# Six key units of the second batch ahead of the expert's weights, and a later place in the order for readers of transferred data

## The chip, the cores and the metric

The kernel runs on one core of a Trainium2 chip. The metric is the device time of one execution in microseconds (us): the median of three runs of the kernel before is 1073.74 us (1071.4 to 1074.57). All rows of a profile in this document come from one profiled execution. PE is TensorE's matmul, PEld its weight load, DVE is VectorE, ACT ScalarE, POOL GpSimd, SP SyncE (which here only issues transfers). The granted clock (PEclk) is the share of TensorE's full speed that the throttle let through.

## The reference

Four batches of 11456 tokens with 128 channels. 49 agent vectors of each batch attend to the keys and average the values; each token then attends to the 49 averages. The result goes through a mixture of eight experts, of which each token takes the one with the largest gate logit.

```python
def _attn_ref(q, k, v, agents):
    a2k = sm(agents, k)                  # softmax of scale * a @ b.T
    agent_v = a2k @ v                    # 49 x 128 per batch
    q2a = sm(q, agents)
    return q2a @ agent_v

def _moe_ref(x, w_gate, w_output_gate, w1, w2):
    logits = x @ w_gate
    e_idx = np.argmax(logits, axis=1)
    ...
    for e in range(E):
        mask = e_idx == e
        h = np.maximum(x[mask] @ w1[e], 0.0)
        out[mask] = gate_w[mask, None] * eom[mask, e, None] * (h @ w2[e])
```

## The kernel before, in words

**Units and tiles.** A batch is cut into 12 units of 1024 tokens (the last has 192). Each batch has 12 key units (k), 12 value units (v) and 12 query units (q). A k unit is eight f32 products of the keys with the agents (`ks`), whose running maximum goes to DVE and whose scores are kept; a v unit is eight products `av` with the exponentials; a q unit is eight products `qs`, then maximum, exponential, a split into two f16 parts (`e16`), one transposing transfer into `x1`, four copies of 19 rows of `x1` into the four row groups of `x2`, and the gate logits `lg` from `x1`. When all values of a batch are averaged, `fold` finds the expert that most tokens take (`ei`), reads that number into SP, loads its two weight matrices (`w1t` in two halves, then `w2t`), multiplies the averages into the first (`aw`), scales and splits the results into `w` (the work of `first`) and the second matrix into `vv` (the work of `second`). The main loop then runs over 92 tiles of 512 tokens, 23 a batch: `h` products with `w` (`mm1`), `hh` on ACT and the remainder `hl` on DVE (`relu`), `y` products with `vv` (`mm2`), the sum into `os`, a multiplication on POOL and a store.

**The tokens of other experts** ("left" tokens) are gathered afterwards: `left_table` and `left_index` build their list with transfers into one buffer (`bigs` in the profile: rows of `ppid` by SP, rows of `cumd` and `efd` by gathers on POOL), DVE counts in that buffer, and 14 left tiles of 128 tokens each (two at first, then eleven of the first three batches, then one of the last batch) load their expert's weights and run `let`, `lx`, eight `lh` and eight `ly` products with ACT between them; a scatter on POOL writes them over the output. They are meant to run between the products of the last batch.

**What sets the order.** There is no order written by hand. The program is written out by generators ("streams") with priorities, and a planner, class `Clock`, keeps an estimated time for each engine and for each tile the time at which it is ready or read for the last time. `Clock.can` lets a request pass when its operands' estimated times have come, for some engines with an additional delay (`LATE`: 600 ns on PE, 800 on POOL, 2000 on SP, 0 on ACT and DVE), which holds only after the main loop has started and not where the writer is the asking engine. Up to now a transferred tile counted as written by the engine that issued its transfer. These estimates decide only in which order instructions stand on each engine; on the chip each engine runs its list in order and waits where an operand is not there, so an instruction placed too early holds up all behind it. `idle` fills an estimated gap of PE, before the main loop starts, with products on a constant (`warm`); next to the f32 products before the start stand fillers too (`beside`).

**Loads.** `loads` issues k, q and v units in the order of `ITEMS` into eight places of half a megabyte; a place comes free when the products of its unit are done. From item `FIRST_ITEMS` on (28 before) it also waits while `picking` is true, which `fold` sets before it reads the expert's number and clears once the expert's transfers are issued.

The lines that the change touches are `Clock.at` and `Clock.can`, the transfer branch of `Engine.emit` (line 174 on), `fold`, `second`, `order`, `FIRST_ITEMS`, the end of `main_stream`, and two pauses of the left tiles.

Of the kernel before, what the change touches and what calls it, by code (L numbers as in the profile page):

```python
# [47 lines left out]


class Clock:  # L50

# [6 lines left out]
    def __init__(self):  # L58
        self.vt = dict.fromkeys(("PE", "ACT", "DVE", "POOL", "SP", "DMA"), 0.0)
        self.ready, self.read, self.writer, self.before = {}, {}, {}, {}  # L60
        self.slots = [1, 2]
        self.pe = 0.0
        self.psum = set()

        self.apart = {"out"}
        self.recent = []
        self.started = False

    def now(self):
# [7 lines left out]

    def at(self, ins, outs=(), eng=None, late=0.0):

        t = 0.0  # L80
        for x in ins:
            if x.name not in self.apart:
                t = max(t, self.ready.get(x.name, 0.0) + (0.0 if self.writer.get(x.name) in (eng, "PE") else late))
        for x in outs:
            n = x.name
            if n in self.apart:
                continue
            if self.writer.get(n) != eng:
                t = max(t, self.ready.get(n, 0.0))
            t = max(t, self.read.get(n, 0.0), self.free_at(n))  # L90
        return t
# [5 lines left out]
    def can(self, req, prio):  # L97
        eng, ins, outs, kind = req
        now = self.now()
        t = self.at(ins, outs, eng, self.LATE[eng] if self.started and (prio > 0 or eng == "PE") else 0.0)  # L100
        if eng == "PE":
# [34 lines left out]
class Engine:  # L136
# [40 lines left out]
    def emit(self, op, ins, outs, a, k):  # L177
        if "dma" in op:
# [7 lines left out]
            for x in outs:  # L186
                c.ready[x.name] = max(c.ready.get(x.name, 0.0), q + (2500.0 if turned else 950.0))
                c.writer[x.name] = self.name
            for x in ins:
# [53 lines left out]
def agent_attention_top1_moe(ctx, tc, qT, kT, v, aT, wg, wo, w1, w2, cst, out):  # L243
# [422 lines left out]
    def fold(b):  # L666
# [36 lines left out]
        yield from SY.q.dma_start(w2t, w2[bass.ds(er, 1)].rearrange("a p f -> p (a f)"))  # L703
        picking[0] = False
        aw, marks = [], []
# [25 lines left out]
        release(mark)  # L731
        yield from SY.q.dma_start(avnd[b], avn[0:A])

    def gates(b, ad):
# [70 lines left out]
    def second(b, w2t):  # L805

        sq = wk.tile([P, 2], F32, name=f"sq2{b}", tag="sq")
        vvs = []
        for hf in range(2):
# [157 lines left out]
    def order():  # L967
        items = [("k", 0, u) for u in range(NU)] + [("q", 0, 0), ("q", 0, 1)] + [("v", 0, u) for u in range(NU)]
        for b in range(B):
            qs = [("q", b, u) for u in range(2, NU)]  # L970
            if b + 1 < B:
                qs += [("q", b + 1, 0), ("q", b + 1, 1)]
                ks = [("k", b + 1, u) for u in range(NU)]
                vs = [("v", b + 1, u) for u in range(NU)]
# [8 lines left out]
        return items  # L983

    MIX = [(3, 0)] * 4 + [(0, 0)] + [(0, 2)] * 6 + [(0, 0)]
    ITEMS = order()
    UNIT = {"q": q_unit, "k": k_unit, "v": v_unit}
    FIRST_ITEMS = 2 * NU + 4

# [102 lines left out]
    def main_stream():  # L1092
# [3 lines left out]
        while m2 < len(second_):  # L1096
# [23 lines left out]
            else:  # L1120
                idle()
        while streams:
            idle()
# [94 lines left out]
    def left_index(ph, i, n, nm, got=None):  # L1218
# [78 lines left out]
        for k in range(n):  # L1297
# [3 lines left out]
            if got:  # L1301
                got(k, clk.ready[big.name] + (4000.0 if n > 1 else 1000.0), ti, tg, ef, oa)
            yield from pause(1500.0 if n > 1 else 0.0)
# [18 lines left out]
    def pause(ns):  # L1322

        t = clk.now() + ns
        while clk.now() < t:
            yield None
# [63 lines left out]
    def left_static():  # L1390
# [3 lines left out]
        def fronts():  # L1394
            for i, (ph, k) in enumerate(todo):
# [4 lines left out]
                av, w1t, w2t = yield from left_load(ph, ti, kk, f"{ph}_{k}")  # L1400
                yield from pause(max(clk.ready[x.name] for x in (av, w1t, w2t)) - clk.now() + 2000.0)
                xs = yield from left_front(f"{ph}_{k}", ef, av)
# [119 lines left out]
```

## Time and profile before

| | before |
|---|---|
| median of three runs | 1073.74 us (1071.4 to 1074.57) |
| the profiled execution's own time | 1073.62 us |
| its span | 1071.6 us |
| its mean granted clock | 0.984 |
| PE busy | 1033.2 us |
| DVE busy | 859.9 us |
| ACT busy | 592.6 us |
| POOL busy | 275.2 us |
| bytes moved | 147.13 MB |

The span runs from the first to the last instruction; 2.0 us of the execution's own time lie around it. A busy PE isn't a PE at its peak: at half the granted clock a product takes longer and PE still counts as busy, so a stretch is to be read with both columns, busy time and PEclk. In the rows of a timeline the columns are start, duration, engine, line, operation, output<-input, shape and count, and in brackets the idle time just before and what ended it. Nearly all instructions are written from one helper line (L193), so rows are told apart by tile names, whose numbers are left out. An f32 product shows as two passes (x2).

### The profile page before, as it was taken

The numbers are of one execution on the slowest core, as the hardware profiler recorded it, in microseconds if no ns is written. First come the engines' busy times: TensorE is split into PE (matmuls) and PEld (weight loads), VectorE is DVE, ScalarE is ACT, GpSimd is POOL, SyncE is SP. The second block draws the span as 40 slices with busy tenths as digits, with TensorE's granted clock in tenths as the row PEclk, the third lists the DMA queues.
The fourth block names the chain that finished last, engine by engine and source line by source line (L and its number), as shares of the span: only waits on it lengthen the run. The fifth ranks groups of instructions, "written<-read, shape, count | busy, mean of one in ns | idle before, by whom it ended". The sixth has DMA issues, their size and how long they took to land. (4 is left out here: it accounts for less than half of the span.)

```text
span 1071.6 us, 27654 instructions
## 1 busy us (share of the span) xinstructions
PE 1033.2 (96%) x10671; PEld 840.9 (78%) x10671; DVE 859.9 (80%) x2344; ACT 592.6 (55%) x1396; POOL 275.2 (26%) x440
## 2 busy tenths in 40 slices
PE   9989899999999999999999999999899999999996
PEld 9977777788788877778788788777677676788885
DVE  2738699888988898888988888989989978877551
ACT  2325456565755665556755665556645554655552
POOL 0301123222121232232121232321123263521121
PEclk9999899999999999999999999999999998999998
DMA  8785854444557444453466544446232732644430
GB/s 293 231 213 156 193 117 146 125 122 136 133 141 197 141 134 112 119 147 116 111 185 166 153 125 119 129 123 171 73 75 56 168 92 78 149 136 130 131 124 28
DMA packets 108818, 147.13 MB, mean 137 GB/s; under 512 B 61128, under 2 KB 71548, under 8 KB 108682
## 3 DMA queue, kind: packets, MB, share of 16 engines
q1 hardware_dynamic: 107338, 143.83, 48.4%
q0 software_dynamic: 1344, 1.49, 0.8%
q8 instruction: 85, 1.39, 0.5%
q14 instruction: 51, 0.42, 0.1%
HBM read 91.86 MB, written 35.17 MB: 119 GB/s over the span
## 5 line engine op out<-in xcount | busy, mean ns | idle before, releaser
L193 PE MATMUL y<-vv,hh 128*128 128x256 f16 (+1 forms) x2880 | 593.0, 275 | 4.3 <-DVE w L193 3.1
L193 PE MATMUL y<-vv,hl 128*128 128x128 f16 (+1 forms) x2880 | 532.7, 220 | 3.3 <-DVE hl L193 2.5
L193 DVE SCALAR_TENSOR_TENSOR hl<-h,hh 128x512 f16<-128x512 f32 (+1 forms) x736 | 447.0, 667 | 85.3 <-ACT hh L193 84.2
L193 ACT ACTIVATE hh<-h 128x512 f16<-128x512 f32 (+1 forms) x736 | 372.2, 591 | 231.3 <-PE h L193 231.0
L193 PEld LDWEIGHTS <-hh 128*128 128x128 f16 (+1 forms) x2880 | 284.7, 99 | 67.0 <-issue 37.1
L193 PEld LDWEIGHTS <-hl 128*128 128x128 f16 (+1 forms) x2880 | 320.7, 112 | 10.9 <-DVE hl L193 6.2
L193 PE MATMUL h<-x_ld,w 128*128 128x512 f16 (+1 forms) x1472 | 289.4, 379 | 12.1 <-DVE hl L193 11.5
L193 PEld LDWEIGHTS <-w 128*128 128x128 f16 x1472 | 98.3, 103 | 105.0 <-issue 84.7
L193 POOL TENSOR_TENSOR os<-os,smt 128x512 f32<-128x512 f32 (+1 forms) x92 | 94.3, 1025 | 234.8 <-issue 168.9
L193 ACT COPY ys<-y 128x256 f32<-128x256 f32 x180 | 67.4, 374 | 99.6 <-PE y L193 97.4
L193 PEld LDWEIGHTS qs<-at,q_ld 128*128 128x128 f32 x720 | 112.0, 190 | 7.0 <-DVE km_m L193 0.3
L193 PE MATMUL qs<-at,q_ld 128*128 128x50 f32 x720 | 114.0, 245 | 0.0
L193 PE MATMUL ks<-at,k_ld 128*128 128x50 f32 x720 | 111.4, 257 | 2.2 <-DMA k_ld<-kT 2.2
L193 PEld LDWEIGHTS ks<-at,k_ld 128*128 128x128 f32 x720 | 109.2, 195 | 5.5 <-DMA k_ld<-kT 3.1
L193 PE MATMUL av<-ev,v_ld 128*128 128x50 f32 x720 | 110.7, 251 | 0.0
L193 PEld LDWEIGHTS av<-ev,v_ld 128*128 128x128 f32 x720 | 107.6, 191 | 1.8 <-ACT ev L193 0.2
L193 DVE TENSOR_TENSOR os<-y,ys 128x256 f32<-128x256 f32 x180 | 75.0, 417 | 30.3 <-ACT ys L193 22.4
L193 POOL TENSOR_TENSOR e<-ef,e 128x392 f16<-128x392 f32 (+1 forms) x48 | 41.8, 870 | 151.9 <-ACT e L193 93.4
L193 POOL TENSOR_TENSOR ev<-S,km_o 128x400 f32<-128x400 f32 (+1 forms) x44 | 41.1, 935 | 150.7 <-PE av L193 108.6
L193 POOL TENSOR_SCALAR smt<-lT,i 128x8 f32<-128x8 f32 (+1 forms) x48 | 14.8, 309 | 130.6 <-DVE lT L193 109.9
L193 PEld LDWEIGHTS <-idle_x 128*128 128x128 f16 x305 | 45.9, 158 | 2.7 <-DVE idle_x L193 1.1
L193 PE MATMUL lh<-lxs,lw 128*128 128x128 f32 x224 | 42.9, 276 | 0.0
(200 smaller groups left out, 1041.3 us busy)
## 6 DMA issues: line engine op xcount, KB each, us to landing
q_ld<-qT SPq DMA_DIRECT2D x44, 512.0 KB
v_ld<-v SPq DMA_DIRECT2D x44, 512.0 KB
out<-os SPq DMA_DIRECT2D x88, 256.0 KB
k_ld<-kT SPq DMA_DIRECT2D x43, 512.0 KB
lw<-w SPq DMA_DIRECT2D x28, 512.0 KB
efd<-ef SPq DMA_DIRECT2D x44, 200.0 KB
x_ld<-x_ld SPq DMA_DIRECT2D x176, 38.0 KB
w1t<-w SPq DMA_DIRECT2D x8, 256.0 KB
```

What stands on the lines that cost most here:

```text
L193: return getattr(self.eng, op)(*a, **k)
```

## The change

Five things are changed.

1. **Order of loads.** Six k units of batch 1 (`PRE = 6`) stand in `ITEMS` directly behind the values of batch 0, and `FIRST_ITEMS` is 32, so that they are loaded and scored without waiting for the expert. Before, `q0_2` and one k unit stood there.
2. **End of picking.** `picking` is cleared by a stream of its own, `picked`, when the planner expects `w2t` to have arrived, not when its transfer is issued.
3. **Order of the weights' preparation.** In batch 0 `second` begins when both parts of `w` have been written out.
4. **A transfer is a writer of its own.** A transferred tile's writer is now "DMA". After the start every reader of such a tile is placed 1500 ns (`LANDS`) behind the estimated arrival, on DVE and ACT too; at the end of the main loop this margin becomes 0. Since "DMA" is never the asking engine, the planner also lets a second transfer into the same tile wait for the first one's estimated arrival: the two halves of `w1t` and of the first k unit, the four copies into `x2`, the two parts of `wgo`, the rows gathered into the left tokens' buffer. No such wait is in the program itself; only the places in the order change. `lg` is asked for only after the fourth copy into `x2` has been issued (`q_rest`).
5. **Pauses of the left tiles** are 2000 ns shorter, or 1000 where one tile is gathered alone.

```diff
+LANDS = 1500.0
...
-    def at(self, ins, outs=(), eng=None, late=0.0):
+    def at(self, ins, outs=(), eng=None, late=None):
...
-                t = max(t, self.ready.get(x.name, 0.0) + (0.0 if self.writer.get(x.name) in (eng, "PE") else late))
+                w = self.writer.get(x.name)
+                if w == "DMA" and late is not None:
+                    more = self.margin
+                else:
+                    more = 0.0 if w in (eng, "PE") else late or 0.0
+                t = max(t, self.ready.get(x.name, 0.0) + more)
...
-        t = self.at(ins, outs, eng, self.LATE[eng] if self.started and (prio > 0 or eng == "PE") else 0.0)
+        t = self.at(ins, outs, eng, (self.LATE[eng] if prio > 0 or eng == "PE" else 0.0) if self.started else None)
...
-                c.writer[x.name] = self.name
+                c.writer[x.name] = "DMA"
...
-        picking[0] = False
+        spawn(picked(w2t), -1)
...
+    def picked(w2t):
+
+        yield from pause(clk.ready[w2t.name] - 950.0 - clk.now())
+        picking[0] = False
...
+        while b == 0 and len(state[b]["w"]) < 2:
+            yield None
...
+        items += [("k", 1, u) for u in range(PRE)]
...
-                ks = [("k", b + 1, u) for u in range(NU)]
+                ks = [("k", b + 1, u) for u in range(0 if b > 0 else PRE, NU)]
...
+    PRE = 6
...
-    FIRST_ITEMS = 2 * NU + 4
+    FIRST_ITEMS = 2 * NU + 8
...
+        clk.margin = 0.0
...
-                got(k, clk.ready[big.name] + (4000.0 if n > 1 else 1000.0), ti, tg, ef, oa)
+                got(k, clk.ready[big.name] + (2000.0 if n > 1 else 0.0), ti, tg, ef, oa)
...
-                yield from pause(max(clk.ready[x.name] for x in (av, w1t, w2t)) - clk.now() + 2000.0)
+                yield from pause(max(clk.ready[x.name] for x in (av, w1t, w2t)) - clk.now())
```

Three places show how the order moves. Line numbers differ because lines were added; the numbers at the ends of names are running numbers of buffers.

**SP's list between the values of batch 0 and its expert** (k1_0 is the first key unit of batch 1, x10_1 and x20_1 are x1 and x2 of batch 0's query unit 1, ei0 the expert's number). Before:

```order
L193 DMA q0_2_ld_737<-qT 128x1024
L193 DMA x20_0_ld_651<-x10_0_ld_634 19x1024 x4
L193 DMA_TRANSPOSE x10_1_ld_751<-e16_1_84 128x8x128
L193 DMA k1_0_ld_769<-kT 128x1024
L193 DMA x20_1_ld_757<-x10_1_ld_751 19x1024 x4
L696 TENSOR_LOAD ei0_929
L193 ISA
L193 DMA w1t0_938<-w1 128x512
L193 ISA
L193 DMA w1t0_938<-w1 128x512
L193 ISA
L193 DMA w2t0_941<-w2 128x1024
```

After, where four more key units, k1_0 to k1_3, and the first two of the four copies into x20_0 stand ahead of these rows:

```order
L203 DMA k1_4_ld_882<-kT 128x1024
L203 DMA k1_5_ld_902<-kT 128x1024
L203 DMA x20_0_ld_697<-x10_0_ld_687 19x1024 x2
L203 DMA_TRANSPOSE x10_1_ld_952<-e16_1_84 128x8x128
L706 TENSOR_LOAD ei0_971
L203 ISA
L203 DMA w1t0_982<-w1 128x512
L203 ISA
L203 DMA w1t0_982<-w1 128x512
L203 ISA
L203 DMA w2t0_1039<-w2 128x1024
```

The key units and the second transposing transfer now stand directly ahead of the expert's number, and the copies into x2 are no longer one group of four but are spread between loads. On PE the scores of k1_0 to k1_3 and five of the eight of k1_4 now stand ahead of the first `aw`; before, only q0_2 and k1_0 stood there. At the very beginning of PE's list 17 `warm` products now stand between the second and the third key unit, where there were none, and between the values and the start the `warm` products are 14 where there were 29.

**DVE's reading of the eleven gathers for the left tokens** (`bigs0_2<-bigs0_2,lppxs0_2` reads the eleven gathered rows; hl82_0 is a remainder of tile 82, os75 the output of tile 75). DVE before:

```order
L193 SCALAR_TENSOR_TENSOR hl76_4_16026<-h76_1_0_16002,hh76_4_16025 128x512
L193 SCALAR_TENSOR_TENSOR hl76_5_16029<-h76_1_1_16010,hh76_5_16028 128x512
L193 SCALAR_TENSOR_TENSOR hl76_6_16031<-h76_1_2_16014,hh76_6_16030 128x512
L193 SCALAR_TENSOR_TENSOR hl76_7_16033<-h76_1_3_16019,hh76_7_16032 128x512
L193 TENSOR_TENSOR os75_16005<-y75_1_16038,ys75_1_16087 128x256
L193 TENSOR_TENSOR bigs0_2_15045<-bigs0_2_15045,lppxs0_2_15567 128x990
```

DVE after:

```order
L203 SCALAR_TENSOR_TENSOR hl82_0_16919<-h82_0_0_16903,hh82_0_16918 128x512
L203 SCALAR_TENSOR_TENSOR hl82_1_16922<-h82_0_1_16908,hh82_1_16921 128x512
L203 SCALAR_TENSOR_TENSOR hl82_2_16924<-h82_0_2_16910,hh82_2_16923 128x512
L203 SCALAR_TENSOR_TENSOR hl82_3_16926<-h82_0_3_16912,hh82_3_16925 128x512
L203 TENSOR_TENSOR os81_16975<-y81_0_16896,ys81_0_16976 128x256
L203 TENSOR_TENSOR bigs0_2_15386<-bigs0_2_15386,lppxs0_2_16231 128x990
```

POOL's list around the last of these gathers, before:

```order
L193 TENSOR_TENSOR os74_15703<-os74_15703,smt3_2_14862 128x512
L193 DMA bigs0_2_15045<-cumd0_100,lrus0_2_15685 128x90
L193 TENSOR_SCALAR smt3_6_15996<-lT3_6_15991,i123_13761 128x8
L193 COPY ef3_6_15472<-lT3_6_15991 128x8
L193 TENSOR_TENSOR oht_1_96<-oh3_6_15959,ndom3_13423 128x8x8
L193 DMA bigs0_2_15045<-cumd0_100,lrus0_2_15685 128x90
L193 DMA out<-bigs0_0_14369,ltu0_0s0_0_14909 34368x128
L193 DMA bigs0_2_15045<-cumd0_100,lrus0_2_15685 128x90
L193 TENSOR_TENSOR os75_16005<-os75_16005,smt3_3_15231 128x512
```

POOL after:

```order
L203 DMA bigs0_2_15386<-cumd0_100,lrus0_2_16376 128x90 x2
L203 TENSOR_TENSOR os79_16631<-os79_16631,smt3_5_15909 128x512
L203 DMA bigs0_2_15386<-cumd0_100,lrus0_2_16376 128x90 x3
L203 TENSOR_TENSOR e16_2_85<-ef3_10_16848,e16_2_85 128x8x49
L203 CAST e16_2_85<-ef3_10_16848 128x8x30
L203 TENSOR_TENSOR os80_16814<-os80_16814,smt3_5_15909 128x512
L203 TENSOR_TENSOR os81_16975<-os81_16975,smt3_6_16084 128x512
```

Before, the last gather stood ahead of tile 75's multiplication on POOL, and DVE read the rows directly behind tile 75's last sum. Now the last gather stands between the multiplications of tiles 79 and 80, and DVE reads the rows in tile 82, more than a tile later; the whole chain of the left tokens stands about five tiles later in the last batch.

**The end of PE's list** (y91 is the last tile of the main loop; in lh0_12_1 the numbers are phase, left tile and half, and lh1_0 is the one left tile of the last batch). Before, the last rows ahead of the end:

```order
L193 MATMUL ly1_0_19147<-lw21_0_18937,lh1_0_0_19126 128x128
L193 LDWEIGHTS hl91_7_19042
L193 MATMUL y91_0_19100<-vv3_1_13658,hl91_7_19042 96x128
L193 MATMUL ly1_0_19147<-lw21_0_18937,lh1_0_0_19126 128x128 x3
L193 MATMUL ly1_0_19147<-lw21_0_18937,lh1_0_1_19143 128x128 x4
```

After:

```order
L203 MATMUL y91_0_19042<-vv3_1_13692,hl91_7_18972 96x128
L203 MATMUL ly0_11_19076<-lw20_11_18875,lh0_11_1_19072 128x128 x2
L203 MATMUL lx0_12_19102<-let_sb0_12_19096,lav0_12_19021 128x128
L203 MATMUL lh0_12_0_19130<-lxs0_12_19111,lw10_12_19023 128x128 x4
L203 MATMUL lh0_12_1_19137<-lxs0_12_19111,lw10_12_19023 128x128 x4
L203 MATMUL ly0_12_19145<-lw20_12_19025,lh0_12_0_19135 128x128 x4
L203 MATMUL ly0_12_19145<-lw20_12_19025,lh0_12_1_19142 128x128 x4
L203 MATMUL let1_0_19154<-kc_71,bigs1_0_18502 49x128
L203 MATMUL lx1_0_19162<-let_sb1_0_19156,lav1_0_19124 128x128
L203 MATMUL lh1_0_0_19166<-lxs1_0_19164,lw11_0_19126 128x128 x4
L203 MATMUL lh1_0_1_19173<-lxs1_0_19164,lw11_0_19126 128x128 x4
L203 MATMUL ly1_0_19180<-lw21_0_19128,lh1_0_0_19171 128x128 x4
```

Before, seven products of the last left tile stood behind the last product of the main loop; now nearly all of the last two left tiles stand there.

More of the change, by code (lines that the diff above doesn't have):

```diff
@@ L67, in __init__ @@
         self.started = False
+        self.margin = LANDS
     def now(self):
```

## The prediction

> **What bounds the kernel now.** I read the page's first two parts, then the waits of PE and DVE, then tables by stretch around each wait, then the timeline there. The page first: busy time by engine, and the granted clock in 40 slices of 26.8 us.
>
> ```profile
> PE 1033.2 (96%) x10671; PEld 840.9 (78%) x10671; DVE 859.9 (80%) x2344; ACT 592.6 (55%) x1396; POOL 275.2 (26%) x440
> PEclk9999899999999999999999999999999998999998
> ```
>
> PE bounds the whole: of 1071.6 us only 38.4 are idle, part of them before the first load lands and behind the last product. A new order cannot shorten the products, so what it can win are PE's gaps and the half clock that follows them. The waits of PE, largest first (total, times, longest):
>
> ```profile
> PE h L193 <- DVE hl L193: 11.5, 33, 3.6
> PE lg L193 <- DMA x_ld<-e: 3.7, 1, 3.7
> PE y L193 <- DVE w L193: 3.1, 1, 3.1
> PE ks L193 <- DMA k_ld<-kT: 2.2, 1, 2.2
> ```
>
> Four places carry most of it. The table by stretch shows busy times and clock there, and the left tokens' stage as a whole (800 to 840):
>
> ```profile
> core 0: us, PE busy (x) PEld busy (x) DVE busy (x) ACT busy (x) POOL busy (x), PEclk, DMA share, GB/s
> 76.00:86.00 10.00, 10.00 (x74) 9.37 (x73) 7.39 (x19) 5.85 (x12) 1.51 (x2) 0.66 0.89 340
> 126.00:134.00 8.00, 6.57 (x51) 4.72 (x52) 3.12 (x14) 2.83 (x8) 0.00 (x0) 0.59 0.78 256
> 752.00:760.00 8.00, 7.15 (x47) 4.82 (x47) 6.61 (x22) 4.36 (x11) 1.23 (x2) 0.79 0.05 17
> 798.00:808.00 10.00, 8.29 (x64) 5.13 (x62) 8.64 (x25) 2.85 (x7) 1.69 (x2) 0.83 0.33 78
> 884.00:896.00 12.00, 9.31 (x56) 5.29 (x56) 9.44 (x22) 2.65 (x6) 0.76 (x1) 0.72 0.02 7
> 800.00:840.00 40.00, 36.55 (x358) 26.45 (x358) 36.69 (x108) 21.77 (x52) 13.11 (x22) 0.96 0.27 63
> ```
>
> A stretch at clock c costs its length times (1 - c) beside its gap, where PE has work throughout: 76 to 86 lost 10 x 0.34 = 3.4 us although PE was busy in all of it, 126 to 134 lost 8 x 0.41 = 3.3.
>
> **Part by part: the start.** ACT's copies of scores in the opening and the steps from the expert's number to the first `y` (columns: start, duration, engine, line, operation, count, and in brackets the idle time before and its releaser):
>
> ```profile
> 14.30 0.49 ACT L193 COPY S<-ks 128x400 f32<-128x400 f32 x1 [1.65 <-PE ks L193]
> 16.44 0.49 ACT L193 COPY S<-ks 128x400 f32<-128x400 f32 x1 [1.65 <-PE ks L193]
> ...
> 63.83 0.15 DVE L193 TENSOR_SCALAR ei<-gm 128x1 int32<-128x1 f32 x1
> 65.93 0.94 SPq L193 DMA_DIRECT2D w1t<-w  x2
> 67.51 0.33 SPq L193 DMA_DIRECT2D w2t<-w  x1
> 69.17 2.81 PE L193 MATMUL aw<-w1t,avd 128*128 128x512 f32 x6 [0.20 <-DMA w1t<-w]
> 71.82 0.50 PE L193 MATMUL mw_r<-sq,ones 128*128 128x1 f32 x4
> 74.23 0.63 ACT L193 ACTIVATE vv<-w2t 128x512 f16<-128x512 f32 x1 [3.84 <-DMA w2t<-w]
> 75.53 0.42 PE L193 MATMUL ks<-at,k_ld 128*128 128x50 f32 x2 [2.25 <-DMA k_ld<-kT]
> 82.75 2.24 PE L193 MATMUL warm<-idle_x 128*128 128x256 f16 x10
> 85.03 0.38 PE L193 MATMUL h<-x_ld,w 128*128 128x512 f16 x1
> 87.72 0.27 PE L193 MATMUL y<-vv,hh 128*128 128x256 f16 x1
> ```
>
> In the opening ACT waits for PE and a unit takes 16.44 - 14.30 = 2.14 us, so more fillers there lengthen it. The order has 17 more, and two more beside them; at half clock a `warm` took 0.224 us (2.24 / 10), so 0.11 at full clock: 19 x 0.11 = 2.1 us. The expert's number moves from 63.83 to 66.0, the issue of `w1t` from 65.93 to 68.1. It landed 3.24 us after its issue (69.17), so 71.3 now, or up to 3 us later if the last two key units (two of 512 KB at the 340 GB/s of the row 76 to 86) still fill the queue. PE meanwhile has k1_0 to k1_3 and five eighths of k1_4, 4.6 x 2.14 = 9.9, and 1 us of other products: it comes to `aw` at about 74.3, so that even a late `w1t` is hidden. By 71.82 - 69.17 = 2.65 before and some 2.2 now (nothing else of PE lies between), `mw_r` moves from 71.82 to 76.5, 4.7 us later. Against that, ACT's 3.84 us wait for `w2t` goes, and `second` stands behind `w`: with ACT free for the halves of `w`, I get the first `h` at 84.3 and the first `y` at about 88 against 87.72. The new wait of `second` holds back only `vv` on ACT; behind it stands the first `y`, and that is in the 88.
>
> What has been gained by then is work done ahead. Six k units and 3/8 of a q unit are through, where five units were. A f32 product in the main loop costs PE 0.16 us:
>
> ```profile
> 120.52 0.32 PE L193 MATMUL ks<-at,k_ld 128*128 128x50 f32 x2
> 120.68 0.22 PE L193 MATMUL y<-vv,hl 128*128 128x128 f16 x1
> ```
>
> That is 8 x 0.16 = 1.3 us a unit, so 1.4 units are 1.8 us less in the main loop. Sum of the start: +0.3 - 1.8, taken as **-1**. Ends: -4, if ACT's whole 3.84 us is won; +3.4, if another gap brings the half clock of 76 to 86 into the part that now decides.
>
> On that clock the Trainium skill ("TensorE: Matmul & The Clock Gate", "Part 1: The HAM clock gate (the "warmup" mystery)") says that the gate falls to half only after an idle window of about 3.4 us. By this trace a gap of 2.25 us, at 75.53, was enough. By the page the start would carry no such risk and the upper end would be 0; by the row it stays.
>
> **Part by part: `lg` behind the first `x1` of the main loop.** Here the transfer was read too early by far:
>
> ```profile
> 119.03 2.29 SPq L193 DMA_TRANSPOSE x_ld<-e  x1
> 127.43 0.24 PE L193 MATMUL lg<-gs,x_ld 128*128 128x36 f16 x2 [3.68 <-DMA x_ld<-e]
> ```
>
> It landed 8.4 us after its issue, and PE stood 3.68 us. `lg` is now asked for after four copies that the planner spaces out (about 2.3 us each), plus 1.5 us of margin: some 8 us later in PE's list, which exceeds 3.68. The gap goes, and with it most of the half clock after it (of 3.3 us in the row 126 to 134 I take 2.5, as part lies in the gap itself): **-6.2**. At the worst the planner finds other work to put too early and nothing is won: 0.
>
> **The expert of batch 3** (752.85, row "PE y <- DVE w", 3.12 us). The half clock in 752 to 760 is 8 x 0.21 = 1.7, together 4.8. The two halves of `w1t` are spread, and more `y` now stand ahead of those that need the new `vv`. The wait is for DVE's `w`, not a transfer, so not all of it need go: **-3**, between -4.8 and 0.
>
> **The left tokens' tables** (800 and 884). The waits of DVE and of PE in the two stretches:
>
> ```profile
> DVE bigs L193 <- DMA out<-os: 3.4, 1, 3.4
> ...
> PE h L193 <- DVE hl L193: 1.7, 4, 1.0
> ...
> DVE bigs L193 <- DMA bigs<-cumd,lrus: 6.2, 1, 6.2
> ...
> PE h L193 <- DVE hl L193: 3.8, 2, 3.6
> ```
>
> DVE stands before the gathered rows, with PE's next `hl` queued behind it. On PE the two cost 1.7 + 3.8 of gap and 10 x 0.17 + 12 x 0.28 = 5.1 of clock: 10.6. But DVE is the full engine of this stage (36.69 us of 40 in 800 to 840), so no more comes back than DVE's own idle time, 3.4 + 6.2 = 9.6. DVE now reads the second set more than a tile after its last gather: **-9.5**, between -12 and -3 (only the first one's wait).
>
> **The end.** The left tokens now come about five tiles later, and two left tiles stand behind the last product of the main loop, where seven products stood:
>
> ```profile
> 1054.41 0.27 ACT L193 COPY lxs<-lx 128x128 f32<-128x128 f32 x1 [1.26 <-PE lx L193]
> ...
> 1059.19 1.78 PE L193 MATMUL ly<-lw,lh 128*128 128x128 f32 x14
> 1061.06 0.37 ACT L193 ACTIVATE bigs<-ly,bigs 128x128 f32<-128x128 f32 x1 [1.30 <-PE ly L193]
> ```
>
> A product is 1.78 / 7 = 0.254 us. A left tile alone is 16 of these, 4.1 us, and with the copies between (two of 0.27, an `lh` on ACT, `let`, `lx`) some 5.3: two are 10.7 against 2.3 before (1059.13 to 1061.43). About 26 products, 6.7 us, leave the main loop for it. 10.7 - 2.3 - 6.7 = 1.7, and with gaps between small products the clock may fall (2 us more): **+2.7**, between +1.7 and +3.7.
>
> **New waits.** The order changes everywhere; the trace before has none of the gaps it may bring. By the nearest rows a gap with its clock costs 4.8 to 6.2. I allow one small one, **+3**, between 0 and +8.
>
> **Sum.** The profiled execution took 1073.62 us (1071.6 of span, 2.0 around it), as the median of 1073.74. 1073.6 - 1 - 6.2 - 3 - 9.5 + 2.7 + 3 = 1059.6, so **1060**.
>
> **The rivals.**
> *Some waits go, others come* (1066 to 1071). For it: 11.5 us of PE's waits on `hl` are 33 small ones, which no margin on transfers touches; a reader moved back meets the next engine. Then -6 for `lg`, -3 for the left tokens, +2.7 and +3 or more remain.
> *It doesn't do what it says* (1070 to 1077). A margin of 1.5 us is small against a landing of 8.4, as at 119.03; where the estimate is off by more than the margin, a reader waits just as before at its new place, and the end's +2.7 cancels the rest. Against it: at both places by name the new order has more than the margin between.
> *Slower: the chain to `x2` starves the main loop* (1080 to 1100). The copies went out together:
>
> ```profile
> 94.61 2.48 SPq L193 DMA_DIRECT2D x_ld<-x_ld  x4
> ```
>
> Now they stand apart on SP, with loads between that wait for places. `h` needs all four. If the chain's lead over `h`, one or two tiles of 10.6 us (1059 - 85 over 92), falls under the some 7 us which spreading adds (4 x 2.3 - 2.5), each of the first units costs a stall of up to 7 and 3 of half clock; one to three such units less the gains give 1080 to 1100. Against it: in PE's waits above no `h` stands behind a transfer.
> *More than I take* (below 1051): the left tokens' whole 10.6, batch 3's 4.8, the start's 4, no new wait.
>
> **How the numbers follow.** The forecast (1051 to 1066) gets 0.50, more than that 0.05, the first rival 0.20, no effect 0.14, the slower one 0.11. A measurement of this kernel can tell about 0.3%, 3.2 us, from no change: faster is below 1070.5, slower above 1077. Faster: 0.50 + 0.05 + 0.18 = 0.73; within: 0.02 + 0.13 = 0.15; slower: 0.01 + 0.11 = 0.12. The range leaves out the slower rival, the case below 1051 and 0.04 of "no effect": **1051 to 1074**, which takes in the bounds of the terms, save all of them at one end together.
>
> **What would show it.** Right: no wait of PE for `x1` over 1 us and a clock over 0.95 near 120 to 135; no DVE wait over 2 us for `bigs`; `ei` near 66, first `y` between 85 and 91; about 10 us between the last main-loop `y` and the last `ly`. Wrong: `h` waiting for `x_ld` in the first twenty tiles; a new gap over 3 us with a clock near 0.5 behind it; `aw` waiting over 3 us for `w1t`; PE's waits in sum still above 15 us.

## The result, and the profile after

The changed kernel takes 1047.78 us (median of 4 runs, 1047.25 to 1048.62), the kernel before beside it 1074.15 (4 runs, 1071.4 to 1076.06): a ratio of 0.9757, 95% interval 0.9734 to 0.978. It is faster, as forecast, but by 26 us and not 14, and it lies below the range's low end of 1051. The profiled execution took 1047.73 us, its span is 1046.0.

The page of the changed kernel, parts 1 and 2, busy time by engine and the granted clock in 40 slices:

```profile
PE 1021.1 (98%) x10690; PEld 834.0 (80%) x10690; DVE 871.6 (83%) x2344; ACT 591.4 (57%) x1396; POOL 273.2 (26%) x440
PEclk9999999999999999999999999999999999999998
```

PE is busy 12.1 us less, with nothing left out: the same products ran at full clock, where some ran at half before. PE's idle time in the span fell by 13.5 us (38.4 to 24.9). The waits of PE that are left, the three largest (total, times, longest), and DVE's largest:

```profile
PE h L203 <- DVE hl L203: 3.6, 17, 0.2
PE y L203 <- DVE qz L203: 3.1, 4, 0.9
PE warm L203 <- DVE idle_x L203: 1.1, 1, 1.1
...
DVE hl L203 <- ACT hh L203: 45.5, 59, 2.5
```

No wait of PE for a transfer is left, nor DVE's for `bigs`, and none of PE's is longer than 1.1 us. DVE waited 84.2 us for `hh` before; that it waits 39 us less was not forecast.

Where the time went is read from both traces cut at the same places: at the first `h` of each batch and at the end of PE's last product. The kernel before, by stretch (length, busy times and counts, clock):

```profile
0.00:85.03 85.03, 80.95 (x809) 76.58 (x810) 41.76 (x121) 24.35 (x55) 13.60 (x28) 0.96 0.81 248
85.03:329.90 244.87, 237.41 (x2505) 191.62 (x2504) 213.21 (x596) 142.93 (x340) 58.96 (x105) 0.99 0.53 140
329.90:562.59 232.69, 230.33 (x2469) 187.00 (x2468) 204.48 (x549) 140.97 (x330) 57.51 (x97) 1.00 0.50 139
562.59:793.46 230.87, 225.72 (x2380) 179.82 (x2378) 205.82 (x566) 138.39 (x322) 56.35 (x95) 0.99 0.47 126
793.46:1060.97 267.51, 258.77 (x2519) 205.88 (x2517) 194.65 (x515) 145.62 (x348) 87.79 (x118) 0.98 0.41 114
1060.97:1071.56 10.59, 0.00 (x0) 0.00 (x0) 0.00 (x0) 0.37 (x1) 1.00 (x1) 0.66 0.06 16
```

The changed kernel, the same six:

```profile
0.00:84.41 84.41, 82.50 (x858) 78.45 (x859) 40.27 (x115) 23.71 (x55) 12.56 (x26) 1.00 0.78 227
84.41:318.71 234.30, 230.88 (x2476) 187.75 (x2476) 218.81 (x586) 142.88 (x339) 59.42 (x104) 1.00 0.59 155
318.71:549.72 231.01, 229.20 (x2469) 186.24 (x2468) 212.04 (x550) 140.16 (x331) 57.10 (x96) 1.00 0.51 140
549.72:774.57 224.85, 222.40 (x2370) 177.98 (x2369) 210.11 (x570) 136.99 (x323) 55.24 (x92) 1.00 0.50 129
774.57:1037.23 262.66, 256.10 (x2527) 203.53 (x2525) 190.38 (x527) 147.26 (x350) 87.87 (x121) 1.00 0.40 115
1037.23:1045.96 8.73, 0.00 (x0) 0.00 (x0) 0.00 (x0) 0.37 (x1) 0.97 (x1) 0.68 0.03 7
```

Length less PE busy is PE's gap. From stretch to stretch the lengths change by -0.6, -10.6, -1.7, -6.0, -4.9 and -1.9, together -25.6. Gaps ahead of PE's last product fell from 27.8 to 16.2 us; the half clock there, summed from the records of the clock (half of 27.3 us), fell from 13.7 us to nothing. Gap and half clock are 25.3 of the 25.6.

The places that the prediction named, in the changed kernel. The start:

```profile
66.96 0.14 DVE L203 TENSOR_SCALAR ei<-gm 128x1 int32<-128x1 f32 x1
...
67.84 1.35 SPq L203 DMA_DIRECT2D w1t<-w  x2
...
74.50 1.94 PE L203 MATMUL aw<-w1t,avd 128*128 128x512 f32 x4
76.28 0.50 PE L203 MATMUL mw_r<-sq,ones 128*128 128x1 f32 x4
...
84.41 1.35 PE L203 MATMUL h<-x_ld,w 128*128 128x512 f16 x8
...
87.16 0.27 PE L203 MATMUL y<-vv,hh 128*128 128x256 f16 x1 [0.15 <-DVE vv L203]
```

`aw` does not wait for `w1t`, and the steps stand within a microsecond of the forecast (66.0, 68.1, 74.3, 76.5, 84.3, 88). The wait of `lg`: a transposing transfer behind the start of the main loop, and the first `lg` that reads what it brings:

```profile
113.91 1.27 SPq L203 DMA_TRANSPOSE x_ld<-e  x1
131.10 0.21 PE L203 MATMUL lg<-gs,x_ld 128*128 128x36 f16 x2
```

The trace leaves the units' numbers out, so they are counted along the lists of SP and PE: this is unit 3. It is read 17.2 us after the issue; the `lg` at 115.61, close behind the transfer, still read unit 2, issued at 98.44. The wait of before was unit 4's, the third that the main loop issues: its `lg` was reached 4.7 us behind the issue (127.43 - 3.68 - 119.03), and the data came 8.4 us behind it. Now unit 4 is issued at 130.35 and read at 142.66, 12.3 us later, without a wait. Over all 48 units the shortest time from issue to first reader is 12.1 us, where it was 4.8. And the end, first before, then after (the store of the last tile, then the last scatter of left tokens):

```profile
1060.98 0.33 SPq L193 DMA_DIRECT2D out<-os  x1
...
1063.54 1.00 POOL L193 DMA_INDIRECT out<-bigs,ltg_0s  x1 [2.59 <-SPq L1457]
```

```profile
1037.32 0.37 ACT L203 ACTIVATE bigs<-ly,bigs 128x128 f32<-128x128 f32 x1 [1.30 <-PEq L1479]
1037.96 0.97 POOL L203 DMA_INDIRECT out<-bigs,ltg_0s  x1 [4.45 <-ACT bigs L203]
```

Before, the scatter waited 2.59 us for the store of the main loop's last tile, which it may overwrite. Now that store is 8 us old when the last left tile is done, and the scatter follows ACT at once.

### The profile page after: what moved, and what is told of

It is laid out like the page before. It is cut to its first block, busy times and chain, and to the rows that moved or that the text cites. A ratio compares the mean times of both kernels' runs of the same rounds, so it can differ in the third digit from the quotient of the medians.

```text
span 1046.0 us, 27720 instructions
## 1 busy us (share of the span) xinstructions
PE 1021.1 (98%) x10690; PEld 834.0 (80%) x10690; DVE 871.6 (83%) x2344; ACT 591.4 (57%) x1396; POOL 273.2 (26%) x440
## 5 line engine op out<-in xcount | busy, mean ns | idle before, releaser
L203 DVE SCALAR_TENSOR_TENSOR hl<-h,hh 128x512 f16<-128x512 f32 (+1 forms) x736 | 447.1, 667 | 49.3 <-ACT hh L203 45.5
L203 PE MATMUL h<-x_ld,w 128*128 128x512 f16 (+1 forms) x1472 | 284.7, 376 | 4.8 <-DVE hl L203 3.6
L203 PE MATMUL ks<-at,k_ld 128*128 128x50 f32 x720 | 107.8, 255 | 0.4 <-DVE os L203 0.4
L203 PEld LDWEIGHTS ks<-at,k_ld 128*128 128x128 f32 x720 | 104.5, 190 | 2.8 <-DVE os L203 1.6
L203 POOL TENSOR_TENSOR e<-ef,e 128x392 f16<-128x392 f32 (+1 forms) x48 | 41.4, 862 | 150.5 <-ACT e L203 137.4
L203 DVE TENSOR_REDUCE m<-ks 128x50 f32<-128x400 f32 (+1 forms) x44 | 23.8, 541 | 25.3 <-ACT S L203 25.0
L203 ACT COPY S<-ks 128x400 f32<-128x400 f32 (+1 forms) x48 | 22.7, 476 | 36.0 <-PE ks L203 35.9
```

Source lines behind the costliest of these rows:

```text
L203: return getattr(self.eng, op)(*a, **k)
```

## The experiments

All were timed against the kernel before on the same chip, 4 to 10 runs each (the kernel before 7 to 17); since that kernel's median moved between 1071.8 and 1074.7 us, ratios are compared. The table gives the ratio with its interval and, from each profile, the lengths of the six stretches, the half clock ahead of PE's last product, and the time of PE behind the main loop's last `y`. The profiled execution is one of the runs and not always near their median: e4's took 6.6 us more than the median in the table, e14's 4.2 and e3's 2.7 more, e12's 4.6 less. The stretches of these four are to be read with that.

| kernel | us | ratio (95%) | opening | batch 0 | 1 | 2 | 3 | end | half clock | behind last y |
|---|---|---|---|---|---|---|---|---|---|---|
| before | 1074.15 | 1 | 85.0 | 244.9 | 232.7 | 230.9 | 267.5 | 10.6 | 13.7 | 1.6 |
| changed | 1047.78 | 0.9757 (0.9734-0.9780) | 84.4 | 234.3 | 231.0 | 224.9 | 262.7 | 8.7 | 0 | 10.6 |
| e1 | 1058.02 | 0.9865 (0.9821-0.9910) | 85.3 | 237.2 | 231.0 | 224.8 | 268.7 | 8.7 | 3.4 | 28.6 |
| e2 | 1080.77 | 1.0076 (1.0047-1.0106) | 83.9 | 244.8 | 232.7 | 230.8 | 271.7 | 12.2 | 12.0 | 0 |
| e3 | 1063.66 | 0.9911 (0.9883-0.9940) | 84.2 | 239.5 | 231.9 | 226.0 | 271.0 | 11.9 | 6.8 | 0.3 |
| e4 | 1069.01 | 0.9978 (0.9954-1.0002) | 85.2 | 236.9 | 234.8 | 232.6 | 272.0 | 12.2 | 13.7 | 0 |
| e5 | 1059.04 | 0.9868 (0.9839-0.9897) | 79.2 | 239.0 | 232.0 | 226.8 | 267.3 | 12.2 | 3.4 | 0 |
| e6 | 1074.52 | 1.0014 (0.9986-1.0043) | 81.9 | 247.8 | 233.7 | 230.7 | 265.0 | 12.2 | 12.0 | 0 |
| e7 | 1061.50 | 0.9884 (0.9861-0.9907) | 84.9 | 237.2 | 234.2 | 232.5 | 262.4 | 8.8 | 6.8 | 15.2 |
| e8 | 1055.62 | 0.9827 (0.9804-0.9850) | 83.7 | 234.3 | 231.0 | 224.9 | 272.4 | 9.2 | 3.4 | 28.6 |
| e9 | 1054.38 | 0.9833 (0.9799-0.9867) | 82.0 | 242.8 | 231.3 | 224.9 | 264.0 | 8.7 | 1.7 | 10.6 |
| e10 | 1053.05 | 0.9815 (0.9785-0.9845) | 80.8 | 243.1 | 231.3 | 224.8 | 262.7 | 8.7 | 5.1 | 10.6 |
| e11 | 1050.71 | 0.9805 (0.9775-0.9835) | 84.2 | 236.7 | 231.0 | 224.8 | 262.6 | 9.1 | 0 | 10.6 |
| e12 | 1058.11 | 0.9877 (0.9845-0.9908) | 83.5 | 238.6 | 229.6 | 224.5 | 266.5 | 9.1 | 0 | 21.0 |
| e13 | 1053.32 | 0.9829 (0.9788-0.9869) | 79.0 | 239.1 | 232.0 | 226.8 | 265.2 | 8.8 | 1.7 | 11.3 |
| e14 | 1059.85 | 0.9864 (0.9847-0.9882) | 84.3 | 234.3 | 231.0 | 224.9 | 279.2 | 8.7 | 12.0 | 6.5 |
| e15 | 1063.06 | 0.9901 (0.9881-0.9920) | 84.5 | 239.0 | 230.9 | 225.4 | 267.9 | 12.2 | 5.1 | 0 |
| e16 | 1052.31 | 0.9801 (0.9777-0.9826) | 84.6 | 240.8 | 229.6 | 224.5 | 261.2 | 9.2 | 3.4 | 21.1 |
| e17 | 1045.19 | 0.9748 (0.9731-0.9765) | 84.8 | 234.3 | 229.4 | 224.3 | 261.8 | 8.8 | 0 | 10.6 |
| e18 | 1046.63 | 0.9763 (0.9746-0.9780) | 83.5 | 234.4 | 231.0 | 224.9 | 261.9 | 8.8 | 0 | 10.6 |

### Which part: e1 to e4

e1 is the kernel before with part 4 alone, e2 the changed kernel without it. In the others a record of the issuing engine brings back one half of the old rule:

```diff
+                c.issuer[x.name] = self.name
 # e3, no margin
-                w = self.writer.get(x.name)
...
+                w = self.issuer.get(x.name)
+                more = 0.0 if w in (eng, "PE") else late or 0.0
 # e4, no spacing
-            if self.writer.get(n) != eng:
+            if self.issuer.get(n) != eng:
```

> The kernel before with part 4 alone (a transfer as a writer of its own: margin and spacing of second transfers); order of loads, picking, second and the pauses as before. Theory M (the planner's reading of transfers wins most): about 1052 us, since of the 25.6 us by which the profiled spans differ only some 3 lie ahead of the main loop's first units. Theory L (the loads ahead of the expert win most, by removing the start's half clock and by work done ahead): 1066 to 1072. Theory C (any new order loses the few large gaps by chance): 1050 to 1075, with new gaps at other places.

> The changed kernel without part 4 (neither margin nor spacing; loads, picking, second and pauses as changed). Theory M: 1068 to 1072, the waits for x1 and for the gathered rows come back with half clock behind them. Theory L: 1050 to 1055. Theory C: anything from 1050 to 1075.

> The changed kernel with the spacing of second transfers but without the margin of 1500 ns (readers are delayed as before: 600 ns on PE, none on ACT and DVE unless a rule of before says so). Theory M with the margin as its active part: 1058 to 1065, with waits over 1.5 us on transfers again. If the spacing is the active part: 1048 to 1052.

> The changed kernel with the margin but without the spacing of second transfers into a tile. If the margin is the active part: 1046 to 1051 (the opening is 2 us shorter, since the 17 fillers between the second and third key unit go). If the spacing is: 1058 to 1065, with lg waiting for x1 again near 125.

Part 4 alone is worth 1.4% (e1), and the other parts without it lose 0.8% (e2, slower than any of the three theories allowed): all loads and pauses moved, and the waits for transfers stand as before or longer. PE's waits for transfers in e2:

```profile
PE lg L203 <- DMA x_ld<-e: 5.7, 3, 3.0
PE aw L203 <- DMA w1t<-w: 3.6, 1, 3.6
```

So the key units ahead of the weights do not keep `aw` from waiting by themselves, and their number is not what decides: in e2 and in e5 below, 27 of their products stand ahead of the first `aw`, and only in e2 does it wait. What differs is SP's list. In e2, e4 and e7, where the copies into `x2` are not spaced, the last key unit ahead of the weights is issued 4.6 to 4.8 us before `w1t`, and `aw` waits 3.5 to 3.8 us; in e3, e5, e13 and the changed kernel it is 6.9 us, and `aw` does not wait. That loads still under way held up `w1t` fits this but is not shown.

Theory L falls. Theory M holds in its sign, not in its size: 1058 and not 1052, since the start keeps a half clock (3.4 us) and 28.6 us of left tiles stand alone behind the main loop. Of part 4's halves both are needed. Without the margin 1.5% of the ratio is lost (e3), most of it in the last batch and the end (11.5 us) and in batch 0 (5.2). Without the spacing, which looks like a side effect of the new writer's name, 2.2% are lost (e4): 11.5 us in batches 1 and 2, 12.8 in the last batch and the end. That one half alone is the active part falls: e3 lies where it was expected with the margin as that part, e4 above both of its ranges. Two waits of PE in e4 that the changed kernel lacks:

```profile
PE aw L206 <- DMA w1t<-w: 3.5, 1, 3.5
PE y L206 <- DVE w L206: 3.1, 1, 3.1
```

### Which spacing: e5, e6, e7 and e13

The changed kernel, with the rule for second transfers kept for some tiles only:

```diff
-            if self.writer.get(n) != eng:
+            if (self.writer if n.startswith("x2") else self.issuer).get(n) != eng:   # e5
+            ... n.startswith("w1t") ...                                            # e6
+            ... n.startswith("big") ...                                            # e7
+            ... n.startswith(("x2", "big")) ...                                    # e13
```

> The changed kernel, but of all second transfers only the copies into x2 are spaced (e4, with none spaced, took 1069.0; the changed kernel, with all, 1047.8). If the x2 copies are the active part (they carry lg, and with it the small waits of hl on hh in every tile): 1054 to 1058, with DVE's waits on hh near 50 instead of 81 us and batches 1 and 2 shorter by 4 and 1 us. If the halves of w1t are: 1067 to 1069.

> The changed kernel, but only the halves of w1t are spaced. If they are the active part: 1055 to 1058, since e4 lost 3.5 us (aw on w1t) with 3.4 of half clock at the start and 3.1 (y on w) with 3.4 at batch 3's expert, 13.4 in all. If the x2 copies are: 1067 to 1069.

> The changed kernel, but only the gathers and rows for the left tokens are spaced. If they are what shortens the last batch: 1056 to 1060 (e4's last batch and end are 12.8 us longer than the changed kernel's). If the last batch gains from the order elsewhere: 1066 to 1069.

> The changed kernel, but only the copies into x2 and the gathers and rows for the left tokens are spaced, not the halves of w1t, wgo and k0_0. If the two gains add (e5 took 10.0 us off e4's 1069.0, e7 7.5): 1050 to 1053. If the halves of w1t are needed beside them: 1055 or more. If the opening's fillers cost what they seem to (first h at 79.2 in e5 against 84.4): 1047 or less.

Two of them act. The copies into `x2` give 1.1% over e4: the first `h` comes 6.0 us earlier, batches 1 and 2 are 2.8 and 5.8 us shorter, and DVE's waits on `hh` fall from 81.4 to 48.3 us, near the 45.5 of the changed kernel. (e7, without this spacing, has batches 1 and 2 within 0.6 us of e4's, so these two do not come from e4's long profiled execution.) The gathers for the left tokens give 0.9%, all of it in the last batch and the end (-9.7 and -3.4 against e4's profile, which was 6.6 us longer than e4's median, so the ratio is the better measure). Together (e13) they give 1.5%, where 2.0 would have been their sum. The 0.7% that e13 lacks of the changed kernel are about what e10 below loses, in which the halves of `w1t` are spaced and only `wgo` and the first key unit are not; which of the three tiles is needed was not settled. e5 and e7 lie 1.0 and 1.5 us above the ranges expected for them, e13 0.3, e6 5.5.

What the spacing of the `x2` copies does can be seen in all 20 profiles. Without it (the kernel before, e2, e4, e6, e7) the first `lg` of some unit stands 4.8 to 5.4 us behind the issue of its transposing transfer, and each of the five has `lg` waiting for `x1`. With it, in the other fifteen, the shortest such time is 10.7 to 12.1 us and `lg` never waits for `x1`. The margin adds little here: 4.8 to 5.4 (e2, e4) or 11.2 to 12.1 (e3, the changed kernel). So these waits do not go by chance, as theory C had it.

The halves of `w1t` alone give nothing (e6): the wait of `y` for `w` at batch 3's expert is gone there, and `lg` waits instead, in seven places:

```profile
PE lg L206 <- DMA x_ld<-e: 12.8, 7, 4.1
```

In e6 these waits come in spite of the 1500 ns of margin.

### The other parts: e8 to e11

```diff
 # e8, the pauses of before
+                got(k, clk.ready[big.name] + (4000.0 if n > 1 else 1000.0), ti, tg, ef, oa)
+                yield from pause(max(clk.ready[x.name] for x in (av, w1t, w2t)) - clk.now() + 2000.0)
 # e9, the loads of before
+    PRE = 0
+    FIRST_ITEMS = 2 * NU + 4
 # e10, no spacing for k0_ and wgo
+            if (self.writer if not n.startswith(("k0_", "wgo")) else self.issuer).get(n) != eng:
 # e11, second doesn't wait for w
-        while b == 0 and len(state[b]["w"]) < 2:
-            yield None
```

> The changed kernel with the longer pauses of the left tiles as before. By the ledger of e1 against the changed kernel (last batch 268.7 against 262.7 us, five left tiles behind the main loop's end instead of two): 1053 to 1055. If the pauses do nothing: 1047 to 1049.

> The changed kernel with the old order of loads (no key units of batch 1 ahead of the expert's weights, the old number of items that may pass while the expert is picked). If the key units ahead of the weights are what saved the start (the 2.5 us wait for k_ld and the half clock behind it, as e1 still has them): 1051 to 1054. If the start is as long without them: 1047 to 1049. If the order behind it decides: outside both.

> The changed kernel, but the two parts of wgo and of the first key unit aren't spaced, so that the 17 fillers between the second and third key unit of the opening go. If the prediction's price of them (2.1 us, 0.11 each) holds: 1045 to 1046.5. If they are hidden behind loads: 1047 to 1049. If a shifted order decides more than they do: over 1050.

> The changed kernel without the wait of second for both parts of w. If ACT's wait for w2t was on the path of the start: 1051 to 1055 (3.8 us, and half clock if PE runs dry behind it). If it is hidden behind the key units that PE now has: 1047 to 1049.

The pauses, which the prediction gave no term of their own, are worth 0.7%: with the old ones five left tiles and not two stand alone behind the main loop, and the last batch has 3.4 us of half clock. The loads are worth about as much (e9 0.9833 against 0.9757): opening and batch 0 together take 324.8 us and not 318.7. `second`'s wait is worth some 3 us by the medians, 5 by the ratios (e11), at the edge of the first expectation; 2.4 of it stand in batch 0, with no half clock. e8 and e9 lie 0.6 and 0.4 us above the first of their ranges. With the end of picking undone (part 2) the order of every engine's instructions is the same, row for row, so that part does nothing and was not timed.

e10 came out in the third of its cases. Without the 17 fillers the first `h` comes 3.6 us earlier, as the prediction's step says (2.1 by its price). But batch 0 then takes 8.8 us more, with 5.1 of half clock in two places (behind 85.7 and 150.5). The order behind the fillers is another one, and it has waits of the kind that the changed kernel lacks.

### Margin and pauses moved further: e12, e14, e15, e16

```diff
 # e12 and e15
-LANDS = 1500.0
+LANDS = 3000.0    # e15: 600.0
 # e16: LANDS = 3000.0 and
+                    more = min(self.margin, 1500.0) if x.name.startswith(("big", "l")) else self.margin
 # e14
+                got(k, clk.ready[big.name] + 0.0, ti, tg, ef, oa)
+            yield from pause(500.0 if n > 1 else 0.0)
```

> The changed kernel with a margin of 3000 ns instead of 1500. If 1500 is enough and more only makes things late: 1048 to 1053 (left tokens' tables later, more left tiles behind the main loop's end at 5.3 us each, less 4.1 that leave the main loop). If landings still surprise at 1500: below 1047.

> The changed kernel with pauses shorter still (no 2000 ns ahead of a left tile, 500 instead of 1500 ns between its gathers), so that fewer products of left tiles stand behind the main loop's end. If a left tile costs 5.3 us behind the end and 4.1 in the loop: 1045 to 1047. If the tiles then wait for their gathers and loads, as in e2: 1050 or more.

> The changed kernel with a margin of 600 ns instead of 1500. If landings are mostly less than 600 ns later than the planner estimates: 1045 to 1050. If the 1500 are needed: near e3 (no margin on DVE and ACT), 1057 to 1064, with waits on the gathered rows in the last batch.

> The changed kernel with a margin of 3000 ns in the main loop and 1500 for what the left tiles read. If e12's loss (1058.1, 21.0 us behind the main loop's end against 10.6) comes from its late left tiles alone: 1045 to 1048. If the larger margin makes the last batch late by itself: 1052 to 1058.

All four are slower. With 600 ns the time is that of the old rule (e15 0.9901, e3 0.9911), so the size matters. With 3000 batches 1 and 2 gain another 1.8 us, but the left tiles come late (21.0 us behind the main loop) and batch 0 loses 4.3; the median lies 5 us above both ranges, and since the profiled execution was the shortest of four (clock 0.997, the others 0.989 to 0.993), the half clock of the others is in no trace. e16 meant to bring the left tiles forward and did not: 21.1 us still stand behind, so the margin on the tiles for which it was lowered is not what delays them. Four left tiles alone at the end were no loss there, since the last batch is even 1.4 us shorter: what e16 loses is batch 0, 6.5 us longer, with 3.4 of half clock. Its time lies in the range of the second case, but not for the reason given there. e14 moved them further forward (6.5 us behind), and PE stood 10.7 us in the middle of the last batch:

```profile
PE y L203 <- ACT hh L203: 10.7, 1, 10.7
...
ACT ys L203 <- remote: 10.5, 1, 10.5
```

ACT, and DVE with it, stood there while POOL issued eleven gathers, 1.3 us apart; the profile does not name what released them ("remote"), and this is left open.

### A neighbour that is faster: e17 and e18

```diff
                     mains[0] += 1
+                    clk.margin = 3000.0 if 30 <= mains[0] < 58 else LANDS
```

> The changed kernel with a margin of 3000 ns from tile 30 to tile 57 only, 1500 elsewhere; the order at the end is the changed kernel's. In e12 and e16 batches 1 and 2 were 1.4 and 0.4 us shorter with 3000 than in the changed kernel. If that holds where only these tiles have it: 1046 to 1047.3, 0.5 to 1.8 below e18. If it comes from the order ahead of them: as e18.

> The changed kernel itself again, on the chip of e17 and beside it: 1047 to 1049, as in the first measurement. If the chips differ by more than that, the neighbours e5 to e16 cannot be compared by their times alone, only by their ratios to the kernel before.

The larger margin in tiles 30 to 57 alone leaves the end's order as it is and gives 1045.19 us (1044.35 to 1045.42) against 1046.63 (1045.94 to 1047.08) of the changed kernel on the same chip; the five runs of each do not overlap, while the two ratios' intervals do. Batches 1 and 2 are 1.6 and 0.5 us shorter; the 1.4 us by which the median lies below e18's are within the 0.5 to 1.8 expected, the time itself is below the range, as e18's is by 0.4. The gain is small, 0.14%. The repetition's ratio, 0.9763, agrees with the first, 0.9757.

## Why the prediction was too small

**The bound** was right: what was won is PE's gaps and the half clock behind them, 25.3 us. The sum of the terms was 14.0; the trace has 25.6. The mechanism held: every sign that the prediction named for being right came, and none of the signs of being wrong (PE's waits are 14.4 us in sum, where over 15 was the sign; 26.1 before). Most of the terms were too small. Term by term:

**The start**, taken as -1, gave -3.0: the opening is 0.6 us shorter, and 15 more f32 products of units are done in it (30 more passes of `ks` and `qs`), 2.4 us at the prediction's 0.16 each. Every step of its chain was met. It was mis-sized in the work ahead, 11 products against 15 (before, three k units and 1 1/8 q units of that work were through, not five units), and in rounding up for a half clock that did not come back.

**The wait of `lg`**, taken as -6.2, gave -7.5: batch 0 lost 4.0 us of gap and all 3.4 of its half clock, not 2.5. The step of the working, `lg` some 8 us later in PE's list, was met (12.3 us behind the issue, where it was reached at 4.7), only the unit was not the first of the main loop but its third. That both halves of part 4 are needed here is not shown: `lg` waits 5.7 us in sum with neither (e2), nowhere with the spacing alone (e3), and with the margin alone only later (e4, 1.2 us). But the margin is no safeguard: with it and the halves of `w1t` spaced, `lg` waits 4.1 us at this very place (e6, at 128).

**Batch 3's expert**, taken as -3 of 4.8, gave -4.4 (2.7 of gap, 1.7 of clock). The wait for `w` went wholly. The spread halves of `w1t`, which the prediction named, are enough for that (e6), but not needed: the wait is gone in e5 too, where only the copies into `x2` are spaced, and stands in e4 and e7, where neither is.

**The left tokens' tables**, taken as -9.5, gave -8.5 up to the last `y` (gap from 8.7 to 5.4, clock 5.1). The mechanism holds: without the gathers' spacing (e4) or without the margin (e3) the last batch loses this gain, and DVE waits for `bigs` again (6.0 us in e3, 5.1 in e5, which spaces only the copies into `x2`).

**The end**, taken as +2.7, gave about +0.2. From the last `y` to the end of the span it is 19.35 us against 12.21. To ACT's last step it is 11.1 us, forecast as 10.7. But 27 `lh` and `ly` products, 6.9 us, left the main loop for it, the clock did not fall between the small products (the 2 us I had added), and the scatter's wait for the last store went. That last is a saving of 1.9 us that the working did not see; e2, e4, e5, e6 and e15, in which no left tile stands behind the last `y`, all pay 12.2 us there and not 8.7. A left tile behind the main loop's end costs PE gaps but hides the last store.

**New waits**, +3, did not come, and this is the step that failed most. It was an average of what a new order brings, and the neighbours show that the average was not absurd: e8 to e16 differ from the changed kernel in one or two numbers or rules each, and all nine are slower, by 3 to 15 us in their medians (for the smallest, e11 and e16, the intervals of the ratios just touch the changed kernel's), several of them by one or two new gaps with half clock behind them (e10, e14, e16). The changed kernel is an order without such a gap; only one of its neighbours, e17, was faster. That could not be read from the profile of before. The case in which all terms stand at their good ends was among the rivals ("more than I take", with 0.05), and the range left it out ("save all of them at one end together") as if the terms were independent. They are not: with part 4 undone (e2) the wait of `lg`, that for `w` and 12.0 us of half clock are all back together.

Of the 11.6 us by which the sum is short, the new waits are 3.0, the end 2.5 and the start 2.0. The remaining -2.4 us had no term: batch 1 is 1.7 us shorter, batch 2 another 1.6 beside its expert, with DVE waiting less on `hh`. e5 against e4 puts this on the spacing of the `x2` copies. How they shorten it, tile by tile, was not settled.

**The rivals.** "Some waits go, others come" is what the neighbours do, e6 above all, not the changed kernel. "It doesn't do what it says" did not come either: readers now stand 12 us and more behind the issue, the margin being the smaller part of that. The slower rival, `h` starved by its copies, was seen in no run: in none of the 20 profiles does `h` wait for a transfer. What made a kernel slower than before (e2) was another one, `aw` waiting 3.6 us for `w1t` and `lg` for `x1`.

## What to carry to other kernels

Where a planner fixes the order ahead of time, try a later estimated time for the data that transfers bring than for those that engines write, and a time of its own for each transfer into one tile: here the first was worth 1.5%, and the second, which looked like a side effect, 2.2%. That transfers into one tile land one after another is not shown by this; the second works at least in part by setting the readers further back. Price a gap on a clocked engine together with the half clock that may follow it. And before judging one order, ask how its neighbours do: here a change of one or two numbers or rules moved the time by 3 to 15 us.

## What the runs showed of the hardware

The clock can fall to half without a long gap. In every run its changes up to PE's last product lie on one grid of 3.41 us. In e5, the window of that grid ahead of a fall and the one behind it (length, PE busy, clock in the third column from the right):

```profile
81.65:85.06 3.41, 1.86 (x20) 1.76 (x19) 3.38 (x8) 3.02 (x6) 0.00 (x0) 1.00 1.03 413
85.06:88.47 3.41, 3.41 (x18) 2.21 (x18) 3.41 (x17) 0.00 (x0) 0.00 (x0) 0.50 0.95 335
```

PE was idle 1.55 us of that window, in one gap, and the next whole window ran at half. The idle time need not be in one piece: in the kernel before, the window from 798.14 on was idle 1.71 us in gaps of at most 1.04, and the clock fell behind it too. In the changed kernel, the window with the most idle time in the main loop was idle 1.20 us, and the clock stayed:

```profile
920.94:924.35 3.41, 2.21 (x20) 1.06 (x16) 2.57 (x5) 2.59 (x7) 3.08 (x3) 1.00 0.52 173
```

Over all 20 profiles there are 40 such falls from full clock ahead of PE's last product (the ends of products are modelled in the profile, so the idle sums are approximate). Every window in which PE was idle for 1.8 us or more was followed by one (18 falls); between 1.2 and 1.8 us it went either way (17 fell, 17 stayed). Five came after less idle time, four of these ahead of the first `h` of the main loop or just at it, where PE is partly busy with fillers and narrow products. The Trainium skill ("TensorE: Matmul & The Clock Gate", "Part 1: The HAM clock gate (the "warmup" mystery)") gives a window of about 3.4 us, and the grid agrees with it; that the window must be idle as a whole, as the prediction read it, does not agree.
